# One decode step on one core: the loads of x, b2 and b1 go from ScalarE's DMA queue to SyncE's, between the loads of K

## The chip, the cores and the metric

The kernel runs on one core of one Trainium2 chip. The metric is the device time of one execution in microseconds (us), smaller is better. The unchanged kernel took 99.79 us (median of 3 runs, 99.71 to 99.85).

## The reference

The kernel computes one decode step (batch 1, one token, width D = 1024, bfloat16): a residual, sliding-window attention with cached keys and values, and an MLP beside it, both fed from one layernorm.

```python
def _A_ref(x, k_cache, v_cache, wq, wo):          # Hq 32, Hkv 4, Dh 128, Sk 65536
    W = min(4096, max(256, Sk // 4))              # 4096
    q = (x @ wq).reshape(B, Sq, Hq, Dh).transpose(0, 2, 1, 3)
    k = jnp.repeat(k_cache[:, :, Sk - W:, :], rep, axis=1)
    v = jnp.repeat(v_cache[:, :, Sk - W:, :], rep, axis=1)
    p = softmax(einsum("bhqd,bhkd->bhqk", q, k) * Dh ** -0.5)
    o = einsum("bhqk,bhkd->bhqd", p, v)
    return o.transpose(0, 2, 1, 3).reshape(B, Sq, Hq * Dh) @ wo
def _B_ref(x, w1, b1, w2, b2):                    # F 3584
    h = gelu(layernorm(x) @ w1 + b1)
    return h @ w2 + b2
xn = layernorm(x)
return x + _A_ref(xn, ...) + _B_ref(xn, ...)
```

Nearly all of the work is reading: wq and wo are 8 MB each, w1 and w2 7 MB each, the windows of K and V 4 MB each. The vectors that the change touches are small: x and b2 have 2 KB each, b1 has 7 KB.

## The kernel before, in words

The program is written out by hand, engine by engine, with semaphores between them. What matters here is the order of the loads and who waits for them.

**SyncE (SP in the profile) issues all large loads, in this order.** K of groups 0, 1 and 2 (`load_k`, 1 MB each, L221), wq in two halves (4 MB each, `load_chunks`, L155), K of group 3, and w1 whole (7 MB). None of these waits for anything but the start. Then SP waits until VectorE has transposed all of K (`C["kt"]`), since V is loaded into the same buffer KV, and issues V in four loads of 1 MB (L279). Then it waits for the query product (`done["q"]`) and issues w2 in two loads over wq's place; then for w1's product (`done["h"]`) and issues wo in five loads (L288), of which the last three, with the rows from TAIL on, go to KT. The last thing is the store of the result (L380). A load on one queue is cut into pieces that are spread over the core's 16 DMA engines.

**ScalarE (ACT) issues three small loads at its very start**, on its own queue: x and b2 with `row_load` (L164), each as 16 pieces of 64 numbers into one row of XBRP, and b1 (L168) as 28 numbers into each of 128 rows of B1T. After them comes its first activation table.

**What waits for them.** TensorE (PE) waits for x and b2 together (`s_x` at 32), since they count on one semaphore; then it spreads x over 128 rows (L388), and VectorE (DVE) computes the first and second layernorm from PSUM (L236 to L266), up to XZ and YZ, the spread vectors that the products with wq and w1 take. b1 is first read at L336, when w1's product has been transposed back.

**TensorE's order** is x, five small products that open the PSUM banks (L392), the product with wq (in two halves, released through GpSimd at L218 when a half of wq has landed), the scores with the transposed K, the product with w1, the product with V, then w2 and wo in rounds of four rows (`pe_round`), each behind the landing of its load, and a tail for the last rows of wo in KT.

**VectorE** transposes K's four groups (L274) behind the layernorm, each when its load has landed.

**GpSimd (POOL)** builds constants until about 8 us, and then only passes on landings.

Of the kernel before, what the change touches and what calls it, by code (L numbers as in the profile page):

```python
# [17 lines left out]
FC = F // 128  # L18
# [32 lines left out]
def bass_parallel_sum__sliding_block_cached__mixer_channel_mlp__decode_kernel(  # L51
# [17 lines left out]
    pe, dve, act, pool, sp = nc.tensor, nc.vector, nc.scalar, nc.gpsimd, nc.sync  # L69
# [4 lines left out]
    s_x, s_b1, s_v, s_out = (nc.alloc_semaphore(n) for n in ("s_x", "s_b1", "s_v", "s_out"))  # L74
# [13 lines left out]
    def sb(name, shape, d):  # L88
        return nc.alloc_sbuf_tensor(name, shape, d)
# [12 lines left out]
    B1T = sb("B1T", [128, FC], bf16)  # L102
# [50 lines left out]
    def load_chunks(dst, src, chunks, width, semaphores, c0=0):  # L153
        for j, n in enumerate(chunks):
            sp.dma_start(  # L155
                dst[:, c0 * width:(c0 + n) * width].rearrange("p (c n) -> p c n", c=n),
                src[:, c0:c0 + n, :],
            ).then_inc(semaphores[j], 16)
            c0 += n

    XB = XBRP[:, :].rearrange("p (a n) -> p a n", a=16)[:, :, 0:D // 16]

    def row_load(dst, src, semaphore):
        act.dma_start(dst, src.rearrange("o (a n) -> o a n", a=16)).then_inc(semaphore, 16)  # L164

    row_load(XB[0:1], A_x.rearrange("b s n -> (b s) n"), s_x)
    row_load(XB[1:2], B_b2.rearrange("(o n) -> o n", o=1), s_x)
    act.dma_start(B1T[:, :], B_b1.rearrange("(p c) -> p c", c=FC)).then_inc(s_b1, 16)  # L168

    def pool_wait():  # L170
        pool.wait_ge(POOL.sem, POOL.cnt)
# [48 lines left out]
    def load_k(g):  # L220
        sp.dma_start(  # L221
            KV[:, g * 4096:(g + 1) * 4096],
            A_k_cache[0, g, SK - W:SK, :].rearrange("(p i) d -> p (i d)", p=128)).then_inc(s_k[g], 16)

    for g in range(3):
        load_k(g)
    load_chunks(WA, wq_p, WQ_CHUNKS, NQ, s_wq)
    load_k(3)
    load_chunks(W1, w1_p, W1_CHUNKS, F, s_w1)
# [301 lines left out]
```

## Time and profile before

| what | value |
|---|---|
| median of the runs | 99.79 us (99.71 to 99.85) |
| the profiled execution, its own time | 99.69 us |
| its span, first to last instruction | 98.3 us |
| PE busy | 73.4 us (75%) |
| DVE busy | 35.6 us (36%) |
| ACT, POOL busy | 7.0 us, 6.8 us (7% each) |
| read from memory | 39.86 MB, 405 GB/s over the span |
| SP's DMA queue, share of 16 engines | 95.5% |
| ACT's DMA queue, share of 16 engines | 0.1% |

The profile is one execution. The span is the time from its first to its last instruction; what lies around it, 99.69 less 98.3, is 1.4 us. The page lists the busy time of each engine, cuts the span into 40 slices with the busy share of each engine and of the DMA engines in each, follows the work that ended last back to the start (the chain), lists groups of instructions with the idle time before them and what ended it, and gives for each DMA issue the time until its data had landed. "SPq" and "ACTq" are the instructions that issue loads on those engines.

### The profile page before, as it was taken

The numbers are of one execution on the slowest core, as the hardware profiler recorded it, in microseconds if no ns is written. First come the engines' busy times: TensorE is split into PE (matmuls) and PEld (weight loads), VectorE is DVE, ScalarE is ACT, GpSimd is POOL, SyncE is SP. The second block draws the span as 40 slices with busy tenths as digits, with TensorE's granted clock in tenths as the row PEclk, the third lists the DMA queues.
The fourth block names the chain that finished last, engine by engine and source line by source line (L and its number), as shares of the span: only waits on it lengthen the run. The fifth ranks groups of instructions, "written<-read, shape, count | busy, mean of one in ns | idle before, by whom it ended". The sixth has DMA issues, their size and how long they took to land.

```text
span 98.3 us, 1264 instructions
## 1 busy us (share of the span) xinstructions
PE 73.4 (75%) x351; PEld 30.4 (31%) x351; DVE 35.6 (36%) x51; ACT 7.0 (7%) x14; POOL 6.8 (7%) x25
## 2 busy tenths in 40 slices
PE   0026000449995997499999999799979999999982
PEld 0011000023442342134434444333334444443440
DVE  0006998999993791500064500240061000000001
ACT  0500003300000002300004000200000000000001
POOL 6992000000000000000000000000000000000000
PEclk9999999999999999958999999999999999999999
DMA  2999999999999988889999999998899998999990
GB/s 33 387 423 412 457 427 427 427 467 440 427 390 503 653 373 373 373 373 397 413 417 423 420 557 427 453 440 373 350 450 427 427 480 360 440 427 427 392 361 1
DMA packets 2805, 39.88 MB, mean 406 GB/s; under 512 B 498, under 2 KB 500, under 8 KB 756
## 3 DMA queue, kind: packets, MB, share of 16 engines
q1 hardware_dynamic: 2596, 39.85, 95.5%
q10 hardware_dynamic: 208, 0.01, 0.1%
q8 instruction: 1, 0.02, 0.1%
HBM read 39.86 MB, written 0.00 MB: 405 GB/s over the span
## 4 chain that ended last, share of the span: by engine, by line
DMA 60%; PE 30%; SPq 4%; DVE 2%; issue 2%; ACT 1%; POOLq 0%
DMA KT<-in_A_wo_dram 33%; PE PS L395 30%; DMA BIG<-in_A_wq_dram 28%; SPq L288 2%; SPq L221 1%; DVE QBD L305 1%; SPq L155 1%; DVE PT L294 1%; ACT Pb L292 1%; DVE Pb L378 0%; POOLq L218 0%
## 5 line engine op out<-in xcount | busy, mean ns | idle before, releaser
L395 PE MATMUL PS<-BIG,GO 128*128 x96 | 21.4, 379 | 0.6 <-issue 0.5
L395 PE MATMUL PS<-BIG,XZ 128*128 x64 | 16.2, 409 | 3.9 <-POOLq L218 3.9
L274 DVE STREAM_TRANSPOSE KT<-KV 128x4096 bf16<-128x4096 bf16 x4 | 17.5, 4417 | 2.3 <-DMA KV<-in_A_k_cache_dram 2.3
L395 PEld LDWEIGHTS PS<-BIG,GO 128*128 x96 | 9.2, 98 | 11.8 <-issue 2.0
L395 PE MATMUL PS<-BIG,YZ 128*128 x56 | 12.4, 379 | 0.1
L395 PEld LDWEIGHTS PS<-BIG,XZ 128*128 x64 | 6.6, 104 | 14.0 <-issue 8.6
L395 PE MATMUL PS<-KT,QBD 128*128 x32 | 8.8, 442 | 1.4 <-DVE QBD L305 1.4
L395 PE MATMUL PS<-KV,PT 128*128 x32 | 8.2, 377 | 0.6
L392 PE MATMUL PS<-XBRP,HOT 1*128 1x512 bf16 x5 | 2.5, 622 | 8.1 <-DVE XZ L266 8.1
L395 PEld LDWEIGHTS PS<-BIG,YZ 128*128 x56 | 5.4, 96 | 7.1 <-issue 1.3
L378 DVE CAST Pb<-PS 64x256 bf16<-64x256 f32 x1 | 0.4, 417 | 18.2 <-PE PS L395 18.2
L388 PE MATMUL PS<-XBRP,onesb 1*128 1x512 bf16 x2 | 1.0, 602 | 6.8 <-DMA XBRP<-in_B_b_dram 6.8
L395 PEld LDWEIGHTS PS<-KT,QBD 128*128 x32 | 3.5, 110 | 6.6 <-issue 4.0
L395 PEld LDWEIGHTS PS<-KV,PT 128*128 x32 | 3.1, 95 | 5.4 <-issue 3.7
L315 DVE TENSOR_REDUCE MX<-PS 128x1 f32<-128x512 f32 x2 | 1.3, 686 | 9.2 <-PE PS L395 9.2
L236 DVE BATCH_NORM_STATS2 BN<-PS 128x6 f32<-128x512 f32 x2 | 1.3, 689 | 7.8 <-PE PS L388 7.8
L392 PEld LDWEIGHTS PS<-XBRP,HOT 1*128 1x128 bf16 x5 | 0.6, 127 | 9.9 <-DVE XZ L266 9.0
L363 DVE SCALAR_TENSOR_TENSOR QBD<-PS,REC,GMASK 32x512 f32<-32x512 f32 x1 | 0.7, 739 | 6.8 <-PE PS L395 6.8
L336 DVE TENSOR_TENSOR HT<-PS,B1T 128x28 f32<-128x28 f32 x1 | 0.2, 209 | 8.0 <-PE PS L443 8.0
L378 ACT ACTIVATE Pb<-PS 64x256 bf16<-64x256 f32 x1 | 0.4, 380 | 32.2 <-PE PS L395 32.2
L388 PEld LDWEIGHTS PS<-XBRP,onesb 1*128 1x128 bf16 x2 | 0.1, 100 | 6.7 <-POOL FLIP L196 6.7
L395 PE MATMUL PS<-KT,GO 128*32 128x256 bf16 x48 | 1.9, 275 | 0.4 <-DMA KT<-in_A_wo_dram 0.3
(69 smaller groups left out, 32.7 us busy)
## 6 DMA issues: line engine op xcount, KB each, us to landing
BIG<-in_A_wq_dram SPq DMA_DIRECT2D x2, 4096.0 KB, 22.7
BIG<-in_B_w_dram SPq DMA_DIRECT2D x1, 7168.0 KB, 45.5
KV<-in_A_k_cache_dram SPq DMA_DIRECT2D x4, 1024.0 KB, 7.9
KV<-in_A_v_cache_dram SPq DMA_DIRECT2D x4, 1024.0 KB, 18.1
BIG<-in_B_w_dram SPq DMA_DIRECT2D x1, 4096.0 KB, 30.3
BIG<-in_B_w_dram SPq DMA_DIRECT2D x1, 3072.0 KB, 37.2
BIG<-in_A_wo_dram SPq DMA_DIRECT2D x1, 3072.0 KB, 26.1
BIG<-in_A_wo_dram SPq DMA_DIRECT2D x1, 2048.0 KB, 19.1
```

The costliest lines, as they stand in the source:

```text
L155: sp.dma_start(dst[:, c0 * width:(c0 + n) * width].rearrange("p (c n) -> p c n", c=n), src[:, c0:c0 + n, :],).then_inc(semaphores[j], 16)
L221: sp.dma_start(KV[:, g * 4096:(g + 1) * 4096], A_k_cache[0, g, SK - W:SK, :].rearrange("(p i) d -> p (i d)", p=128)).then_inc(s_k[g], 16)
L236: DVE.mark(dve.bn_stats(out=BN[:, 12 * n + 6 * i:12 * n + 6 * i + 6], in_=src[:, 512 * i:512 * i + 512]))
L274: C["kt"] = DVE.mark(dve.transpose(KT[:, i * 4096:(i + 1) * 4096], KV[:, i * 4096:(i + 1) * 4096]))
L288: sp.dma_start(home[:, first:first + n * D], wo_flat[:, c0 * D:(c0 + n) * D]).then_inc(s_wo[j], 16)
L292: C["q32"] = ACT.mark(act.activation(out=Q32, in_=bank(7), func=ACTF.Copy))
L294: C["qtb"] = DVE.mark(dve.transpose(QTB, Q32))
L305: C["d_QBD"] = DVE.mark(dve.tensor_copy(to, of))
L315: DVE.mark(dve.tensor_reduce(out=MX2[:, b:b + 1], in_=S[:, 512 * b:512 * b + 512], axis=AX.X, op=ALU.max))
L388: last = pe.matmul(bank(i), lhsT=onesb[0:1, :], rhs=XB[0:1, 8 * i:8 * i + 8, :])
L392: pe.matmul(bank(n), lhsT=HOT[:, 8:136], rhs=XB[0:1, 0:8, :], start=True, stop=False, skip_group_check=True)
L395: return pe.matmul(to, lhsT=lhsT, rhs=rhs, start=False, stop=False, skip_group_check=True, **place)
```

## The change

The three small loads are issued by SyncE in place of ScalarE, on SP's queue. Their order there is: K of group 0, x, b2, K of groups 1 and 2, b1, and then the two halves of wq, K of group 3 and w1 as before. ScalarE's queue then has no load in this kernel; its first instruction is the table load. The pieces, the destinations and the semaphores are the same. Instructions and waits of PE, DVE and POOL are the same.

```diff
     def row_load(dst, src, semaphore):
-        act.dma_start(dst, src.rearrange("o (a n) -> o a n", a=16)).then_inc(semaphore, 16)
-
-    row_load(XB[0:1], A_x.rearrange("b s n -> (b s) n"), s_x)
-    row_load(XB[1:2], B_b2.rearrange("(o n) -> o n", o=1), s_x)
-    act.dma_start(B1T[:, :], B_b1.rearrange("(p c) -> p c", c=FC)).then_inc(s_b1, 16)
+        sp.dma_start(dst, src.rearrange("o (a n) -> o a n", a=16)).then_inc(semaphore, 16)
...
-    for g in range(3):
+    load_k(0)
+    row_load(XB[0:1], A_x.rearrange("b s n -> (b s) n"), s_x)
+    row_load(XB[1:2], B_b2.rearrange("(o n) -> o n", o=1), s_x)
+    for g in range(1, 3):
         load_k(g)
+    sp.dma_start(B1T[:, :], B_b1.rearrange("(p c) -> p c", c=FC)).then_inc(s_b1, 16)
     load_chunks(WA, wq_p, WQ_CHUNKS, NQ, s_wq)
     load_k(3)
     load_chunks(W1, w1_p, W1_CHUNKS, F, s_w1)
```

## The prediction, made before the changed kernel ran

> **What bounds the kernel now.** I first read the slices and queues on the page, then the chain, to see whether the loads or an engine set the end.
>
> ```profile
> PE   0026000449995997499999999799979999999982
> DMA  2999999999999988889999999998899998999990
> q1 hardware_dynamic: 2596, 39.85, 95.5%
> q10 hardware_dynamic: 208, 0.01, 0.1%
> DMA 60%; PE 30%; SPq 4%; DVE 2%; issue 2%; ACT 1%; POOLq 0%
> ```
>
> The DMA engines are full from the second slice to the last but one. q1 is SP's queue and carries everything but 10 KB; q10 is ScalarE's. The chain is DMA and PE in turn, starting with SP's first issues. Next, the mean rates by stretch of time (stretch, length, busy time and instructions of PE, PEld, DVE, ACT and POOL, clock, DMA share, GB/s):
>
> ```profile
> 0.00:1.50 1.50, 0.00 (x0) 0.00 (x0) 0.00 (x0) 0.00 (x0) 0.68 (x7) 1.00 0.00 0
> 1.50:2.00 0.50, 0.00 (x0) 0.00 (x0) 0.00 (x0) 0.00 (x0) 0.50 (x3) 1.00 0.85 131
> 2.00:3.00 1.00, 0.00 (x0) 0.00 (x0) 0.00 (x0) 0.21 (x1) 0.94 (x3) 1.00 0.50 147
> 3.00:4.00 1.00, 0.00 (x0) 0.00 (x0) 0.00 (x0) 1.00 (x1) 1.00 (x5) 1.00 1.06 442
> 6.00:90.00 84.00, 67.28 (x284) 27.53 (x285) 35.22 (x50) 5.31 (x12) 1.83 (x8) 0.98 1.01 430
> ```
>
> Nothing moves before 1.5 us, the rate is low until 3.0, and from there it holds 430 GB/s. So the end is the start of the stream, plus its bytes at a constant rate, plus a tail. The tail, from the chain in order of time and the timeline:
>
> ```profile
> 64.17 32.09 DMA KT<-in_A_wo_dram
> 96.30 0.32 PE PS L395 x4
> 96.65 0.42 DVE Pb L378
> ...
> 85.31 9.04 PE L395 MATMUL PS<-BIG,GO 128*128 x40
> 94.29 1.06 PE L395 MATMUL PS<-KT,GO 128*32 128x256 bf16 x32
> 95.65 0.95 PE L395 MATMUL PS<-KT,GO 128*32 128x256 bf16 x16 [0.30 <-DMA KT<-in_A_wo_dram]
> ```
>
> wo's last rows land at 96.26 and PE has just caught up, waiting 0.30 us at 95.65. So PE is a close second: the end moves if the loads shift by anything, or PE by more than some 0.3 us. The start, from the timeline and the list of issues:
>
> ```profile
> 0.80 0.58 ACTq L164 DMA_DIRECT2D XBRP<-in_A_x_dram  x1
> 0.80 1.34 SPq L221 DMA_DIRECT2D KV<-in_A_k_cache_dram  x3
> 1.41 0.61 ACTq L164 DMA_DIRECT2D XBRP<-in_B_b_dram  x1
> 2.05 0.71 ACTq L168 DMA_DIRECT2D B1T<-in_B_b_dram  x1
> ...
> XBRP<-in_A_x_dram ACTq DMA_DIRECT2D x1, 2.0 KB, 5.0
> XBRP<-in_B_b_dram ACTq DMA_DIRECT2D x1, 2.0 KB, 5.2
> B1T<-in_B_b_dram ACTq DMA_DIRECT2D x1, 7.0 KB, 7.4
> ```
>
> x lands at 0.80 + 5.0 = 5.8 us, b2 at 1.41 + 5.2 = 6.6, b1 at 2.05 + 7.4 = 9.5. K's groups, asked one by one, start at 0.80, 1.25 and 1.72 and land 4.8, 6.9 and 9.0 later: 5.60, 8.15, 10.72. So x lands as K0 does, although it has its own queue.
>
> **The change part by part.**
>
> *Issue time on SP.* The three issues took 0.58, 0.61 and 0.71 us on ScalarE; with three gaps of 0.04 that is 2.0 us more on SP. K0 stays first. K1's issue moves from 1.25 to 1.20 + 0.04 + 0.58 + 0.04 + 0.61 + 0.04 = 2.51 and ends at 2.93. K0's issue ended at 1.20 and data moved before 2.0, so 0.8 us at most; K1 can move from 3.7 on, and its turn is when K0 is done, at 5.6. That leaves 1.9 us. K2 is issued by 3.4 and ready at 4.2 (turn 8.15), wq ready at 5.4 or, with its own slow 0.77 issue, 5.8 (turn 10.7), and w1, issued last by 6.6, has its turn at 32.6. V's issue waits for DVE's transposes at 37.1, not for SP. Issue time costs nothing, and its cover is K0's transfer.
>
> *The pieces in the stream.* The same 208 packets, which filled 0.1% of 16 engines' span (about 0.1 us of each engine), move from beside K to between K's loads. What they cost beside K: the landings of K0, K1, K2 are 2.55 and 2.57 apart; V's four (issued at 37.11, 37.48, 37.96 and 38.43, landing 15.0, 17.1, 19.1 and 21.1 later) are 2.47 apart. So they already cost 0.08 + 0.10 = 0.18, with rounding of the landings ±0.1. In line they should cost the same. I take 0; bounds -0.1 (if they had hindered K more than their own time) and, above, a stop of the queue at each small load, priced under the second rival.
>
> *The landing of x and b2.* In line behind K0 they land at about 5.6 to 5.8; PE starts with b2, now 6.78, so up to 0.9 us earlier. Nothing follows: XZ is ready at 17.12 and PE's next product waits until 21.09 for wq's first half. DVE's transposes start up to 0.9 earlier and wait longer for K3 (2.30 us now). If x were late, the cover is PE's 21.09 less 18.2, when its last opening product ends: 2.9 us. b1 lands just after K2, near 10.8, and is read at 63.35.
>
> *What leaves ScalarE.* Three issues, 1.9 us, ahead of a table load at 2.79 that is first needed at 9.58. Worth 0.
>
> *SP's first issue without a neighbour.* This decides. K0's issue and x's start together at 0.80. K0's issue took 0.40; SP's first issues after a wait with no issue beside them (V at 37.11, wo at 62.38) took 0.33. wq's first half, issued while ScalarE issued b1, took 0.77 against the 0.43 of other large loads. So issues on two engines do slow each other, and K0's should end 0.07 sooner. The whole stream shifts by that, and wq's landing, from which PE's work follows, with it. I take -0.07, the direct row; bounds 0 and, if ScalarE's issues cause all of the low rate up to 3.0 us, -1.0: by 3.0 us 131 x 0.5 + 147 x 1.0 = 212 KB had moved, where 1.5 us at 430 GB/s would move 645 KB, and the missing 433 KB are 1.0 us.
>
> *Sum.* 99.69 (this execution) - 0.07 + 0 = 99.62. The median of the runs lies 0.10 above the profiled execution, so 99.72 on their scale, which I give as 99.7.
>
> **The rivals.**
>
> *A: the start of the stream gains more.* The low rate ends at 3.0, just after ScalarE's last issue ends at 2.76, and wq's 0.77 shows that issues collide. Against it: the first touches of memory could be slow by themselves, and in the new order x's and b2's issues still fall into 1.2 to 2.5, only on SP. A third to a half of the missing 1.0 us would give 99.2 to 99.5, say 99.4. It decides from 0.2 us on.
>
> *B: slower, the small loads stop SP's queue.* If the queue, in order, waits at a small load until it has gone there and back, the engines stand still; beside K on the other queue that was hidden. The nearest row for a small transfer's way is the store of the result, 0.8 us which SP waits after its issue. x and b2 stand together and b1 alone: two stops of up to 0.8, 1.6 us, or with half of it hidden by the pieces around them 0.8 us, 100.5. It decides when the stops exceed 0.27 us together (the 0.07 gained and 0.2). For it: 16 pieces of 128 bytes and 128 of 56 bytes have never run between large ones in one queue here. Against it: V's loads follow each other in 2.47 us for 1 MB, the full rate, so a load's end does not stop the queue, and wo's last, of 256 KB, lands some 0.66 us after the one before it (63.70 + 31.9 to 64.17 + 32.09), where its bytes at 430 GB/s are worth 0.61. The Trainium skill (DMA: Bandwidth & Descriptors, Anatomy of one DMA) gives every load a fixed cost of some 2.0 us beside its bytes; if that held the queue, three more loads would add an estimated 6.0 us, but V's loads here show no such gap, so I count it as latency that the stream hides.
>
> *C: slower, PE's clock.* PE ran at half clock from 41 to 45 us, after its gap at 38.4 to 41.1; scores ended at 49.87, 0.3 after w1's landing at 49.6. Another such stretch later would cost more than the 0.3 us that PE has at the end. The scores show 4 products per us at half clock and 6 at full: 3.4 us lose about 1.1, less 0.3, so +0.8, 100.5. But the change leaves every gap of PE after 30 us as it is. It decides only if a half-clock stretch starts behind 50 us.
>
> **How the numbers follow.** About 0.2% (0.2 us) is what a measurement of this kernel can tell from no change. My forecast (shift of -0.07, nothing else) has 0.42 and lies within that; its own range is 99.55 to 99.9. A has 0.35. B has 0.20 and C 0.03. So faster 0.35, same 0.42, slower 0.23. The range goes into A to 99.35, which leaves out its far end (0.08), and into B to 100.2, which leaves out its dearer half and most of C (0.12).
>
> **What would show it.** K0 landing before 5.5 us and the first rate of 400 GB/s before 3.0 speak for the shift, and more than 0.2 us of it for A. K0 to K1 at 2.5 to 2.6 us, and K2 to wq's first half at 9.7 as now, show that the small pieces are cheap in line; gaps of 2.8 or more show B. PE's first product should come near 5.9, its wq product still at wq's landing plus 0.7. If the clock falls behind 50 us, it is C. What would make me wrong: a K0 that lands earlier by more than its issue, or a queue that stands still after x, b2 or b1.

## The result and the profile after

The changed kernel is slower: 100.75 us (median of 12, 100.09 to 101.4) against 99.81 (12, 99.69 to 99.92), a ratio of 1.0089 with a 95% interval of 1.0063 to 1.0115. Its executions also spread over 1.3 us, where those of the kernel before lie within 0.25 here. The profiled one took 101.08 us with a span of 99.7, so it lies 0.33 above its median. An execution more than 1.5% above the fastest of its kernel is left out of a ratio as slow, here and in the experiments (101.71 us of x and b2 alone, 101.29 us of K2 late).

Queues, slices and chain of the changed kernel, from the page:

```profile
DMA  3899999999999999999799999999999999999970
GB/s 46 348 367 414 447 434 434 447 421 447 421 404 434 519 483 437 391 391 460 309 408 417 421 483 450 421 434 414 424 444 394 427 444 444 424 411 427 385 272 1
q1 hardware_dynamic: 2804, 39.86, 95.0%
DMA 77%; PE 13%; SPq 6%; issue 1%; DVE 0%
```

ScalarE's queue is gone and its 208 packets are in q1. The bytes are the same. The second and third slices are low (348 and 367 GB/s, 387 and 423 in the kernel before), and the end is ragged: 385 and then 272 in the last two slices with data (392 and 361 before). The chain in order of time:

```profile
5.80 45.16 DMA BIG<-in_B_w_dram
50.96 0.35 issue
51.31 12.45 PE PS L395 x56
...
65.57 32.06 DMA KT<-in_A_wo_dram
97.63 0.04 issue
97.67 0.33 PE PS L395 x3
98.02 0.42 DVE Pb L378
```

w1 lands at 50.96 where 49.6 was, wo's last rows at 97.63 where 96.26 was: 1.4 us late at both, so nothing more is lost after w1. Where it is lost is read from the loads at the start, asked one by one (start plus time to landing, each right to about 0.05 us): K0 lands at 5.90 (5.60 before), b2 at 6.18, **K1 at 9.51 (8.15)**, K2 at 12.03 (10.72), wq's first half at 21.78 (20.39), w1 at 51.0. The step is mostly at K1: K0 itself lands 0.3 late, K0 to K1 takes 3.61 us in place of 2.55, and every later distance is the old one within 0.1. K1's issue in the timeline (start, length):

```profile
2.51 0.58 SPq L217 DMA_DIRECT2D KV<-in_A_k_cache_dram  x1
```

and in the list of issues (the last column is the time from the issue's start to landing):

```profile
KV<-in_A_k_cache_dram SPq DMA_DIRECT2D x1, 1024.0 KB, 7.0
```

So 2.51 + 7.0 = 9.51.

The rates by stretch (the last column is GB/s, the one before it the DMA share), changed kernel:

```profile
4.00:5.00 1.00, 0.00 (x0) 0.00 (x0) 0.00 (x0) 0.00 (x0) 1.00 (x1) 1.00 0.95 369
5.00:6.00 1.00, 0.00 (x0) 0.00 (x0) 0.00 (x0) 0.00 (x0) 0.85 (x4) 1.00 1.18 373
6.00:7.00 1.00, 0.63 (x2) 0.28 (x3) 0.00 (x0) 0.00 (x0) 1.00 (x5) 1.00 0.95 352
7.00:8.00 1.00, 1.00 (x3) 0.28 (x2) 0.59 (x1) 0.00 (x0) 0.83 (x4) 1.00 1.02 410
...
96.00:97.00 1.00, 0.73 (x28) 0.43 (x18) 0.00 (x0) 0.00 (x0) 0.00 (x0) 1.00 0.50 178
```

and the kernel before, in the same stretches:

```profile
4.00:5.00 1.00, 0.00 (x0) 0.00 (x0) 0.00 (x0) 0.07 (x1) 1.00 (x1) 1.00 0.95 402
5.00:6.00 1.00, 0.00 (x0) 0.00 (x0) 0.00 (x0) 0.00 (x0) 0.85 (x4) 1.00 1.02 422
6.00:7.00 1.00, 0.22 (x1) 0.13 (x2) 0.00 (x0) 0.00 (x0) 1.00 (x5) 1.00 0.99 411
7.00:8.00 1.00, 1.00 (x3) 0.28 (x2) 0.18 (x1) 0.00 (x0) 0.83 (x4) 1.00 1.06 430
...
96.00:97.00 1.00, 0.45 (x12) 0.10 (x4) 0.35 (x1) 0.35 (x1) 0.00 (x0) 1.00 0.00 0
```

From 4 to 8 us the changed kernel moves 369 + 373 + 352 + 410 = 1504 KB in place of 1665. The missing 161 KB are 0.4 us at 430 GB/s, yet K1 lands 1.36 late. The two numbers fit if some of the 16 DMA engines lose much and others little, and the packet records of the traces say so. Each load ends with 16 packets of 4 bytes, which I read as one on each engine; for K1 the first and the last of them are 0.31 us apart before the change and 1.62 after it, the mean is 0.5 us later than before and the last 1.3. For w1 the first and the last are 0.27 and 1.56 apart: what is lost at K1 is not made up later. (The records do not name the engine. That the same one stays last is a reading.) A load has landed when its last engine is done, so the end is set by the worst engine. That is why the stretch from 96 to 97 us still moves data, at 178 GB/s, where the kernel before has finished.

The engines are not idle in the low stretches. Their share is 0.95 to 1.18 there, so the packets themselves take longer. Packets of 8 KB, in which K is read, took at most 0.33 us each from 3.2 us on in the kernel before. In the changed kernel 22 of them, between 4.2 and 8.8 us, took 0.40 to 1.24 us. Together they are 6.1 us longer than the usual 0.31 each, or 0.4 us for each of the 16 engines, which is about the missing 161 KB again. The longest (0.9 to 1.24 us) start at 5.36 to 5.41, while the 4-byte packets that end K0, x and b2 run (up to 5.54) and the engines go over to K1.

### The profile page after: what moved, and what is told of

Read it like the earlier page. It is cut to its first block, busy times and chain, and to the rows that moved or that the text cites. A ratio compares the mean times of both kernels' runs of the same rounds, so it can differ in the third digit from the quotient of the medians.

```text
span 99.7 us, 1264 instructions
## 1 busy us (share of the span) xinstructions
PE 72.6 (73%) x351; PEld 30.2 (30%) x351; DVE 35.6 (36%) x51; ACT 7.0 (7%) x14; POOL 6.8 (7%) x25
## 4 chain that ended last, share of the span: by engine, by line
DMA 77%; PE 13%; SPq 6%; issue 1%; DVE 0%
DMA BIG<-in_B_w_dram 45%; DMA KT<-in_A_wo_dram 32%; PE PS L395 13%; SPq L217 2%; SPq L288 2%; SPq L164 1%; SPq L155 1%; SPq L226 0%; DVE Pb L378 0%
## 5 line engine op out<-in xcount | busy, mean ns | idle before, releaser
L395 PE MATMUL PS<-BIG,XZ 128*128 x64 | 17.1, 425 | 4.9 <-POOLq L214 4.7
L395 PE MATMUL PS<-KT,QBD 128*128 x32 | 7.1, 379 | 1.4 <-DVE QBD L305 1.4
L292 ACT ACTIVATE Pb<-PS 128x512 bf16<-128x512 f32 x1 | 0.6, 597 | 22.3 <-PE PS L395 22.3
```

Of the source, the lines that this page charges most:

```text
L395: return pe.matmul(to, lhsT=lhsT, rhs=rhs, start=False, stop=False, skip_group_check=True, **place)
```

## The experiments

Two theories at first. **In line:** small pieces between large ones in one queue make the engines start afresh with the next load. **Late:** it is K1's issue, 2.51 in place of 1.25, that is too late, although K0 is not done before 5.6. In the diffs below the kernel before is the base unless said otherwise. Ratios are to runs of the kernel before on the same chip, with 95% intervals, as they are on record; they need not equal the quotient of the medians.

### Only b1 moved

```diff
-    act.dma_start(B1T[:, :], ...).then_inc(s_b1, 16)
...
     for g in range(3):
         load_k(g)
+    sp.dma_start(B1T[:, :], ...).then_inc(s_b1, 16)
```

> Only b1 is issued on SP, behind K of groups 0, 1 and 2; x and b2 stay on ScalarE's queue, so K1 and K2 are issued as early as before. Theory 1 (small pieces in line make the DMA engines start afresh with the next load): b1 brings 8 pieces for each engine, more than x and b2 together, so wq's first half lands 0.5 to 1.5 us later than before and the time is 100.3 to 101.3. Theory 2 (K1 comes late behind the issues of x and b2): nothing is late, 99.8 within 0.2.

99.91 us (10, 99.74 to 100.54), ratio 1.0007 (0.9987 to 1.0027). 128 pieces of 56 bytes in line cost nothing that can be told here. This speaks against "in line". But the traced execution, 100.33 us, shows that an early issue is no full protection: K1 is issued at 1.25 as before the change and still lands at 1.25 + 7.6 = 8.85, 0.7 late, with no slow packet beyond one of 0.44 us. Such an execution now and then is in the kernel before as well (on this chip 100.11 and 100.31 among 20).

### Only x and b2 moved

```diff
-    row_load(XB[0:1], ...)      # on ScalarE's queue
-    row_load(XB[1:2], ...)
...
+    load_k(0)
+    row_load(XB[0:1], ...)      # on SP's queue
+    row_load(XB[1:2], ...)
+    load_k(1)
+    load_k(2)
```

> Only x and b2 are issued on SP, between K0 and K1; b1 stays on ScalarE. In the trace of the changed kernel K0 to K1 took 3.61 us where 2.55 was, and K2 to wq's first half 9.75 where 9.67 was, so the loss sits before b1. Both theories: most of the loss, 100.4 to 101.1, and K1 landing 0.8 to 1.8 us later than before. If it is under 100.0, b1 is the cause.

101.44 us (4, 100.14 to 101.71), ratio 1.0121 (1.0050 to 1.0192). The whole loss and perhaps more, though four executions are few; the traced one is the longest (101.71), with K1 landing at 10.21. So it is x and b2, or what they do to K1.

### The same three loads, x and b2 one place later

The base is the changed kernel:

```diff
     load_k(0)
+    load_k(1)
     row_load(XB[0:1], ...)
     row_load(XB[1:2], ...)
-    for g in range(1, 3):
-        load_k(g)
+    load_k(2)
     sp.dma_start(B1T[:, :], ...)
```

> As the changed kernel, with x and b2 one place later, between K1 and K2: the same three loads in line, but two loads of K are in the queue before the long issues begin. Theory 1 (small pieces in line): the loss stays, and moves from K0-K1 to K1-K2, 100.4 to 101.1. Theory 2 (K1 late): K1 is issued at 1.25 again and K2 at about 3.0, five us before its turn; no loss, 99.7 to 100.0. The first layernorm starts some 2.4 us later, within the 2.9 us that TensorE waits for wq.

99.87 us (10, 99.73 to 100.25), ratio 1.0014 (0.9998 to 1.0030): the loss is gone, though four of the ten lie between 100.06 and 100.25. x and b2 are in line behind a large load as before, and the next large load, K2, is issued late, at 2.96, but K1 is ahead of it. K1 lands at 8.16 and K2 at 10.66, 2.5 apart, as before the change within the rounding. So small loads in line do not cost it by themselves.

### K1 late, nothing small in line

```diff
     load_k(0)
+    sp.wait_ge(POOL.sem, C["zeros"])      # a memset of GpSimd that ends at 2.78
     load_k(1)
     load_k(2)
```

> The kernel before, with x, b2 and b1 on ScalarE's queue, but SP waits after K0 for a memset of GpSimd that ends at 2.78, so K1 is issued at about 2.8 in place of 1.25, a little later than in the changed kernel (2.51). No small piece is in SP's queue. Theory 1: no loss, 99.8 within 0.2. Theory 2: K1 lands 1 us or more late and the time is 100.4 to 101.4.

100.66 us (5, 100.0 to 101.02), ratio 1.0071 (1.0032 to 1.0109). K1 is issued at 2.82 and lands at 9.22. Its rates:

```profile
4.00:5.00 1.00, 0.00 (x0) 0.00 (x0) 0.00 (x0) 0.00 (x0) 1.00 (x1) 1.00 1.10 403
5.00:6.00 1.00, 0.00 (x0) 0.00 (x0) 0.00 (x0) 0.00 (x0) 0.85 (x4) 1.00 1.06 280
6.00:7.00 1.00, 0.62 (x2) 0.27 (x3) 0.00 (x0) 0.00 (x0) 1.00 (x5) 1.00 0.95 386
```

The same dip, at the end of K0 (280 GB/s where 422 was), with SP's queue holding large loads alone. So a late K1 by itself makes the loss. The DMA share of the dip is 1.06: again the engines are not idle, and again packets are slow. Between 3.2 and 10 us 27 packets of 8 KB took 0.40 to 1.10 us, the two longest at 4.87 and 4.96, just behind the first 4-byte packets that end K0 (4.80 and 4.86).

### How late is too late

A smaller dose, x alone before K1, b2 between K1 and K2, b1 behind K2, all on SP:

```diff
+    load_k(0)
+    row_load(XB[0:1], ...)      # on SP's queue, as the next
+    load_k(1)
+    row_load(XB[1:2], ...)
+    load_k(2)
+    sp.dma_start(B1T[:, :], ...)
```

> A smaller dose: on SP's queue in the order K0, x, K1, b2, K2, b1, so only x's issue stands before K1, which is issued at about 1.87 (1.25 in the kernel before, 2.51 in the changed one, 2.82 where K1 waited for GpSimd). If the loss grows with how late K1 is issued, it lies between: 99.9 to 100.5, K1 landing 0 to 0.7 us late. If there is an edge between 1.9 and 2.5, no loss: 99.8 within 0.2. If any small piece between K0 and K1 costs it, 100.4 or more.

101.18 us (4, 100.05 to 101.44), ratio 1.0108 (1.0038 to 1.0178). The full loss at half the delay, K1 landing at 9.48. A dose that grows with the delay was not seen; an edge below it, or something about x, was left.

A larger dose, K1 behind a later memset (`C["qbd0"]` marks the one of QBD):

```diff
     load_k(0)
+    sp.wait_ge(POOL.sem, C["qbd0"])       # ends at 5.2
     load_k(1)
     load_k(2)
```

> A larger dose: small loads on ScalarE as before, K1 waits for a memset of GpSimd that ends at 5.2. K0, alone, took 4.8 us from issue to landing, so K1 would land at about 10.0 in place of 8.15 and the time be 101.5 to 102.0. If the loss were a fixed price for a late K1 and did not grow, 100.4 to 101.0.

101.48 us (4, 101.31 to 101.61), ratio 1.0157 (1.0139 to 1.0175); K1 lands at 10.12, 1.97 late. Here the engines stand still for a part of the time (share 0.18 from 5 to 6 us):

```profile
5.00:6.00 1.00, 0.00 (x0) 0.00 (x0) 0.00 (x0) 0.00 (x0) 0.85 (x4) 1.00 0.18 27
6.00:7.00 1.00, 0.73 (x2) 0.28 (x3) 0.00 (x0) 0.00 (x0) 1.00 (x5) 1.00 1.09 131
7.00:8.00 1.00, 1.00 (x4) 0.28 (x2) 0.69 (x2) 0.00 (x0) 0.84 (x4) 1.00 0.77 311
```

K1's issue ends at 5.55, and from there to its landing are 4.57 us, of which its bytes at 430 GB/s are 2.44: 2.1 us are latency that an empty queue lays open. Its first 16 packets start 0.6 to 0.9 us after the issue's end and then take 0.78 to 1.41 us each, where later ones take 0.31. All engines lose alike here (the spread of K1's last packets is 0.35 us), and the executions lie within 0.3 us of each other. So the change, in which the engines' mean at K1 is 0.5 us late and not 1.9 as here, costs more than half as much, since its delay strikes the engines unequally.

K1 in time, K2 late, to see whether only the first loads are sensitive:

```diff
     load_k(0)
     load_k(1)
+    sp.wait_ge(POOL.sem, C["qbd0"])
     load_k(2)
```

> Small loads on ScalarE, K1 in time, K2 waits for the same memset: issued at 5.2, 2.95 us before K1 lands at 8.15. In the changed kernel K1 was issued at 2.51, 3.1 us before K0 lands at 5.6. Theory of the lead (a load must be issued some 3 us or more before the one ahead of it lands, wherever in the kernel): K2 lands 0.5 to 1.4 us late, 100.3 to 101.2. Theory of the start (only the first loads, whose first pieces are slow, are hurt): 99.7 to 100.0.

100.28 us (10, 99.69 to 101.29), ratio 1.0028 (1.0000 to 1.0055). K2's issue ends at 5.55, 2.70 before K1 lands at 8.25. The median just misses the expected range: four of ten executions are under 100.0, six from 100.18 up. In the traced one (100.81) K2 lands at 11.92, 1.2 late, and the dip has moved along:

```profile
6.00:7.00 1.00, 0.17 (x1) 0.13 (x2) 0.00 (x0) 0.00 (x0) 1.00 (x5) 1.00 0.99 411
7.00:8.00 1.00, 1.00 (x3) 0.29 (x2) 0.13 (x1) 0.00 (x0) 0.84 (x4) 1.00 1.59 342
8.00:9.00 1.00, 1.00 (x3) 0.15 (x1) 1.00 (x2) 0.00 (x0) 0.00 (x0) 1.00 0.47 181
```

So it is not a matter of the very first load alone, though the same lead costs less here: K1 with 2.5 us lost 0.9 at the median (K1 late, above), K2 with 2.7 us 0.5, and four of its ten executions nothing. The share of 1.59 at 342 GB/s is again slow packets: 21 packets of 0.42 to 1.46 us.

Lateness without small pieces, at the delay that x alone made, behind an earlier memset (of YZ):

```diff
     load_k(0)
+    sp.wait_ge(POOL.sem, C["yz0"])        # ends at 1.85
     load_k(1)
     load_k(2)
```

> Small loads on ScalarE; K1 waits for an earlier memset of GpSimd and is issued at about 1.9, as where x alone stood before it (1.88, 101.18). Nothing small is in SP's queue. Theory of the lead (K1 must be issued more than some 3.7 us before K0 lands): K1 lands 0.5 to 1.4 us late, 100.3 to 101.3. Theory that at this lateness the small piece in line was needed for the loss: 99.8 within 0.3, and then two causes are at work in the changed kernel.

99.78 us (10, 99.70 to 100.71), ratio 1.0012 (0.9994 to 1.0029). Mostly no loss, though three of ten took 100.11, 100.52 and 100.71, and in the last, which was traced, K1 lands at 9.18. The theory of the lead, with some 3.7 us needed, had 100.3 to 101.3 here and missed. If lateness decides alone, this is near the edge.

Between 1.9 and 2.8, with the memset of XZ cut in two:

```diff
+    C["half"] = POOL.mark(pool.memset(XZ[:, 0:KC * XW // 2], 0.0))
+    C["zeros"] = POOL.mark(pool.memset(XZ[:, KC * XW // 2:KC * XW], 0.0))
...
     load_k(0)
+    sp.wait_ge(POOL.sem, C["half"])
     load_k(1)
     load_k(2)
```

> Small loads on ScalarE; K1 waits for the first half of a memset that GpSimd now does in two, and is issued at 2.2 to 2.4. Nothing small is in SP's queue. K1 issued at 1.88 in this way gave 99.78 (10 executions, three of them 100.1 to 100.7), at 2.82 100.66. If lateness alone decides, this is between, 99.9 to 100.6, with executions of both kinds. If it stays at 99.8 with few late executions, the 101.18 with x before K1 at 1.88 needs the small piece in line as well.

100.79 us (6, 99.84 to 101.17), ratio 1.0115 (1.0099 to 1.0131). K1 issued at 2.36, and a loss of 0.6 to 1.4 us in five of six (the traced one is the sixth, with K1 at 8.46).

x alone before K1, all else as before the change:

```diff
     load_k(0)
+    sp.dma_start(XB[0:1], ...).then_inc(s_x, 16)
     load_k(1)
     load_k(2)
```

> Only x goes to SP, between K0 and K1; b2 and b1 stay on ScalarE, K2 follows K1 at once. K1 is issued at 1.88, as in the run that waited for GpSimd's memset with nothing small in line (99.78). If lateness alone decides, 99.7 to 100.1, most executions under 100. If a small piece in line behind K0 is a second cause, 100.5 to 101.3, as with x and b2 spread over the loads of K (101.18).

100.60 us (6, 100.30 to 100.91), ratio 1.0075 (1.0062 to 1.0089). K1's issue starts at 1.88 as with the early memset, but takes 0.57 behind x's in place of 0.33, and so ends at 2.45 in place of 2.21. By what was expected, this result speaks for a small load in line behind K0 as a second cause. The reading by the end of the issue came after the result, and no run here parts the two: none has K1's issue end at 2.45 without a small load ahead of it, or at 2.2 with one.

Sorted by the end of K1's issue (us; K0 lands at 5.6 to 6.1 in all of them):

| kernel | small loads on SP before K1 | K1's issue ends | time, median | range |
|---|---|---|---|---|
| before | none | 1.67 | 99.81 | 99.69 to 99.92 |
| wait for YZ | none | 2.21 | 99.78 | 99.70 to 100.71 |
| x alone | x | 2.45 | 100.60 | 100.30 to 100.91 |
| x between, b2 and b1 later (4 executions) | x | 2.45 | 101.18 | 100.05 to 101.44 |
| wait for half of XZ | none | 2.69 | 100.79 | 99.84 to 101.17 |
| the change | x, b2 | 3.09 | 100.75 | 100.09 to 101.4 |
| x and b2 alone (4 executions) | x, b2 | 3.09 | 101.44 | 100.14 to 101.71 |
| wait for XZ | none | 3.15 | 100.66 | 100.0 to 101.02 |
| wait for QBD | none | 5.55 | 101.48 | 101.31 to 101.61 |

By the waits alone, in which nothing small is in line, the edge lies between 2.21 and 2.69, which is 3.4 to 2.9 us before K0's undisturbed landing at 5.6. Behind it the median loss is 0.8 to 1.0 us up to 3.15, however late, and 1.4 and 1.6 in the two runs of four executions, whose ranges overlap the others; with the empty queue it is 1.7.

### A longer first load, and K1 on ScalarE

If the lead is what counts, x and b2 may stand right behind the first load, and the next may be as late as in the change, once more is under way. The first of two ways, with the changed kernel as the base:

```diff
-    load_k(0)
+    sp.dma_start(KV[:, 0:8192]..., A_k_cache[0, 0:2, ...]...).then_inc(s_k[0], 16)   # 2 MB
+    s_k[1] = s_k[0]
     row_load(XB[0:1], ...)
     row_load(XB[1:2], ...)
-    for g in range(1, 3):
-        load_k(g)
+    load_k(2)
```

> The changed kernel with its first two loads of K made one of 2 MB: then x, b2, K2, b1 on SP as there. The second large load is issued at 2.5 to 2.6, as K1 was in the changed kernel, and x and b2 are in line right behind the first, but the first lands at about 8.2 and not 5.6. Theory of the lead: it has 5.6 us, no loss, 99.7 to 100.1. If a gap of 1.2 us in issuing, or small pieces behind the first load, cost it by themselves: 100.4 to 101.3.

100.06 us (7, 99.86 to 100.17), ratio 1.0023 (1.0009 to 1.0038). The next large load is issued at 2.56, later than K1 in the change, and lands at 10.96, some 2.5 behind the first: no step, and no packet of 8 KB from 3.2 us on takes over 0.34 us. The 0.27 that is left was there before it, since the 2 MB land at 8.40 where K1 landed at 8.15.

The second:

```diff
     def load_k(g):
-        sp.dma_start(
+        (act if g == 1 else sp).dma_start(
...
     load_k(0)
+    load_k(1)
     row_load(XB[0:1], ...)
     row_load(XB[1:2], ...)
-    for g in range(1, 3):
-        load_k(g)
+    load_k(2)
```

> The changed kernel with K1 issued by ScalarE at 0.8, beside K0 on SP; x and b2 still stand on SP's queue right behind K0, K2 is issued at 2.5 as K1 was there, then b1. Theory of the lead: 2 MB are under way from the start, K2 has some 5 us, no loss: 99.6 to 100.0, and if two loads at once shorten the slow start, up to 0.3 us less than before. If small pieces in line right behind K0 cost it by themselves, 100.4 to 101.

99.88 us (12, 99.71 to 100.31), ratio 1.0008 (0.9995 to 1.0021). x and b2 stand right behind K0 on SP's queue, K2 is issued at 2.64, and there is no loss and no slow packet (at most 0.34 us). The start did not get shorter:

```profile
1.50:2.00 0.50, 0.00 (x0) 0.00 (x0) 0.00 (x0) 0.50 (x1) 0.50 (x3) 1.00 0.96 131
2.00:3.00 1.00, 0.00 (x0) 0.00 (x0) 0.00 (x0) 0.50 (x1) 0.95 (x2) 1.00 0.54 147
6.00:7.00 1.00, 0.00 (x0) 0.00 (x0) 0.00 (x0) 0.00 (x0) 1.00 (x5) 1.00 0.97 410
```

No version here beats the kernel before.

## Why the prediction was wrong

**Issue time on SP: this is the step that failed.** Its times were right to 0.2 us (K1's issue at 2.51 to 3.09, 2.93 forecast), but the conclusion, that K1 has 1.9 us to spare and "issue time costs nothing", was not. I took K1 as ready 0.8 us after its issue, from K0's first data, and its turn as K0's landing. The waits on GpSimd show what its issue may cost: counted to K0's undisturbed landing at 5.6, an issue which ends 2.5 us ahead loses 0.9 us, and one that ends 3.4 us ahead mostly nothing. Two things were missing in the sum. K0's first data said when the first packets started, not when they ran at full speed: the rate was low for 1.5 us more, and the full price of an empty queue is 2.1 us between issue and landing (K1 at 5.2). And a delay need not be shared: the mean rate lost 0.4 us, the worst engine 1.4.

**The Trainium skill here.** DMA: Bandwidth & Descriptors (Issuing engines are not separate DMA queues) says that issuing on several engines saves only the issue time, which is usually small beside the transfer. K1 on ScalarE agrees that nothing else is saved (131 and 147 GB/s up to 3 us, as before). The runs show that the issue time itself can cost 0.9 us when it stands before the second load. The fixed cost of some 2.0 us per load that the Trainium skill gives on the same page (Anatomy of one DMA) stands there for loads issued by GpSimd, which the forecast did not say; the 2.1 us of the empty queue, on SyncE's, are near it. In the forecast I took it as always hidden; the waits show that a short lead does not hide it.

**The pieces in the stream: right for the landing.** K1 to K2 took 2.52 and K2 to wq's first half 9.75, with b1 in line, against 2.57 and 9.67. Moving b1 alone: 1.0007. For the mean of the 16 engines b1 is not quite free: from K2 to wq's first half the mean landing falls back by another 0.35 us in the changed kernel, by 0.05 to 0.33 in the traces of the five experiments with b1 in SP's queue, and by at most 0.04 in the seven without. The last engine of the changed kernel stays 1.3 to 1.5 us late from K1 on, so its time does not show it.

**x and b2: right in effect.** They landed at 5.86 and 6.18 (5.6 to 5.8 forecast), PE's first product began at 6.37, and nothing followed from it.

**SP's first issue without a neighbour: wrong.** K0's issue took 0.40 as before, and the rate from 2 to 3 us was 123 GB/s, no better than 147. The 0.07 was not there. The reading that issues on two engines slow each other does not hold up either: in the changed kernel K of group 3 took 0.66 to issue with no other engine issuing. The low rate at the start does not need ScalarE's issues, so rival A did not come.

**Rival B** had the right side and nearly the right time (100.5), but that was luck: its mechanism, a queue that stops at each small load, is not what the runs show, since with a lead small loads in line stop nothing. The sign that I named for it, K0 to K1 of 2.8 us or more, came (3.61), but it comes as well with nothing small in line (3.3 in K1 late). **Rival C** did not occur: the granted clock was 1.0 throughout. The scores even took 7.1 us in place of 8.8, and it bought nothing, since PE then waited 1.7 us for w1.

**What stays open.** Why some 3 us of lead are needed where an empty queue shows 2.1 us of latency, why the first packets of a load that came late take up to 1.46 us in place of 0.31, and why this strikes the engines so unequally, is not settled. Nor is whether x in line adds anything of its own: behind x, K1's issue ended 0.24 later than behind the early memset.

## What to carry to other kernels

When a kernel is one stream of loads from its first microsecond, count for each issue not when the stream reaches it but how long before the load ahead of it lands; here less than about 3 us before the second load cost 0.9%, though the engines were busy all the time. Small loads in the same queue cost next to nothing as pieces, but x and b2 each cost 0.6 us of issue time, so they belong behind the second or third large load, or on another engine's queue. And when a time grows by more than the mean rate explains, look at the spread between the DMA engines, at the ragged end, and at stretches where the DMA share is full and the rate is low.

## What the runs showed of the hardware that was not expected

A little lateness costs more than half of what a lot costs: K1 issued at 2.36 costs 1.0 us, at 5.22 1.7 us. Packets of 8 KB take 0.31 us in a running stream and up to 1.46 us at the start of a load that came late. The spread between the engines that arises at K1 (1.62 us) is as large at w1, 40 us later (1.56). A large load's issue on SP takes 0.33 after a wait, mostly 0.42 to 0.50 behind a large load, and 0.57 to 0.58 behind one of the small row loads.
